# Hashed attention and a gelu feed-forward on one core: new order of the first loads, VectorE's and GpSimd's work spread anew, six banks at the passage, and a branch that falls through

## Chip, cores, metric

The kernel runs on one core of one Trainium2 chip. The metric is the device time of one execution in microseconds (us). Engines are named as the profile names them: PE is TensorE's matmuls, PEld its weight loads, DVE is VectorE, ACT is ScalarE, POOL is GpSimd and SP is SyncE. A "q" behind the name (SPq) is the engine's sequencer, which issues DMAs, branches and waits on semaphores. "Line 310" or L310 is a line of the kernel's source.

## The reference

```python
# attention: 4 batches, 8 heads, 768 positions, head size 64; proj is 64x6
q_bits = (q @ proj) > 0;  k_bits = (k @ proj) > 0          # six bits per row
mask   = bucket(q_bits)[:, None] == bucket(k_bits)[None]   # same bucket only
scores = where(mask, q @ k.T / sqrt(64), -1e9)
attn   = softmax(scores) @ v
# feed-forward: x is 3072 x 512, w_in 512 x 2048, w_out 2048 x 512
h = x @ w_in
out = (h * sigmoid(1.702 * h)) @ w_out
```

## The kernel before

Heads are handled in 16 pairs. For each pair, k and q are fetched, DVE turns them (`kT`, `qT`), PE forms the **hash** (six projections of every row), DVE makes bit features `f` from it, and DMAs spread them into `kf` and `qf`. PE adds the scores of the real rows and of the features, so that pairs in different buckets get a strongly negative score, ACT takes the exponential, PE multiplies by v, and the denominator is a sum of the exponentials, added on POOL and DVE and then summed across partitions by PE (`dn`).

```python
def featured(n, queues):
    f = ...                                     # DVE: hash -> bits
    for i, x in enumerate("kq"):                # k: both halves, then q
        for c in range(2):
            for j in range(2):
                queues[j].dma_start(out=feats[n % 2][x][...], in_=f[...])

def norm(n, c):                                 # one piece, right after dn
    nc.vector.transpose(rt, dn)                 # frees the one small PSUM bank
    nc.vector.reciprocal(r, ...)
    nc.vector.transpose(rt, r.to_broadcast(...))
    nc.vector.tensor_tensor(x_of(n, c), x_of(n, c), rt, op=Alu.mult)
```

Beside attention, one chunk of `w_in` per pair is converted to the form that the feed-forward multiplies (`convert`: a load into one `raw` buffer, then seven DVE operations, with the addition among them on POOL, and a little ACT). The feed-forward forms each block from seven products instead of eight, as in Strassen's scheme. For that it needs sums of quarters of its operands: `in_sums` for `w_in` (they fill `s_in`), `sums_b` for x.

```python
# start of attention, before
fetch(0, "k"); fetch(0, "q", nc.scalar); fetch_v(0)
turn(0, "k"); turn(0, "q")
hashed(0)
featured(0, (nc.sync, nc.scalar))
measure(0, "k"); measure(0, "q")
...
# at the end: a slow path for inputs too large for the exponential
unsafe = nc.values_load(largest[0:1, 0:1].bitcast(I32)) >= SAFE_BITS
with tc.If(unsafe):
    ...
```

## Time and profile before

| | before |
|---|---|
| median of three first runs | 950.01 us (949.92 to 950.5) |
| span of the profiled execution | 948.2 us |
| third hash starts at | 47.62 us |
| last (16th) hash starts at | 324.33 us |
| first product of the feed-forward to the start of its second task | 15.24 us |
| task 4 of the feed-forward | 12.02 us |
| last DVE sum to the end of the span | 8.50 us |

The rows from "third hash" on come from start times in the timeline; they cut the execution into stretches that can be compared between kernels. A task is one block of the feed-forward, seven products on PE. The timed figure is about 2 us above the span of the same execution.

The prediction shows the lines that carry the reading of this profile. One more view belongs beside it: the windows of the kernel before, in the last third of attention. The columns are the window, then each engine's busy time with its number of instructions, the granted clock of PE, and the DMA engines' share and rate.

```profile
core 0: us, PE busy (x) PEld busy (x) DVE busy (x) ACT busy (x) POOL busy (x), PEclk, DMA share, GB/s
255.00:280.00 25.00, 22.74 (x146) 9.42 (x147) 22.83 (x29) 13.28 (x21) 9.39 (x6) 0.93 0.35 72
280.00:305.00 25.00, 22.75 (x152) 10.16 (x150) 22.89 (x29) 14.09 (x22) 10.23 (x7) 0.97 0.36 72
```

PE has gaps of 2.3 us in each 25 us, DVE is busy for almost 23, and the clock is below 1: here, in the last third of attention, PE waits for DVE.

### The profile page before, as it was taken

Reading aid. Unit: us, or ns where it says so; the run is one execution under the profiler, and the core shown is the slowest. Engines: PE = TensorE matmul, PEld = TensorE weight load, DVE = VectorE, ACT = ScalarE, POOL = GpSimd, SP = SyncE. Lnnn points to the kernel's source line nnn. Section 1 sums busy time; section 2 is a strip of 40 time slices with the busy share of each in tenths; the row PEclk is TensorE's granted clock in tenths of the full one; section 3 lists DMA queues with packets and bytes.
Section 4 is the critical chain, followed back from the end, with each engine's and each line's share of the span. In section 5 each row is a group of like instructions: output and inputs, shape, how many; then the busy total and the mean of one; then the engine's idle time right before and its main releaser. Section 6 shows DMA issues by size and latency. Waiting matters only on the chain.

```text
span 948.2 us, 11379 instructions
## 1 busy us (share of the span) xinstructions
PE 916.5 (97%) x4193; PEld 527.7 (56%) x4193; DVE 548.3 (58%) x753; ACT 299.5 (32%) x480; POOL 194.9 (21%) x122
## 2 busy tenths in 40 slices
PE   3999999999899999999999999999999999999996
PEld 1444444444343443444444444447888888888885
DVE  2678878879999788466866687445232314141410
ACT  2756656656565652233233322221000000000000
POOL 2343344345533345011100005300000000000000
PEclk9999999999999999999999999999999999999998
DMA  7533354433333301233333382328242415130101
GB/s 115 91 77 77 78 103 101 95 78 76 76 77 77 73 24 66 106 125 131 130 132 132 133 310 87 112 83 274 77 146 65 157 58 164 56 123 12 34 11 37
DMA packets 178563, 94.32 MB, mean 99 GB/s; under 512 B 129856, under 2 KB 162112, under 8 KB 178496
## 3 DMA queue, kind: packets, MB, share of 16 engines
q1 hardware_dynamic: 175200, 93.05, 34.8%
q10 hardware_dynamic: 3232, 0.43, 0.5%
q8 instruction: 35, 0.57, 0.2%
q14 instruction: 32, 0.26, 0.1%
q0 software_dynamic: 64, 0.00, 0.0%
HBM read 60.82 MB, written 31.46 MB: 97 GB/s over the span
## 4 chain that ended last, share of the span: by engine, by line
PE 87%; DVE 6%; issue 2%; DMA 2%; SPq 1%; ACTq 1%; POOL 0%; ACT 0%; DVEq 0%; POOLq 0%
PE product L630 31%; PE product L588 30%; PE ps L332 13%; PE av L357 10%; PE dn L375 2%; PE hash L305 1%; DVE acc L347 1%; DMA q<-in_q_dram 1%; SPq L315 1%; DVE acc L348 1%; DVE acc L349 1%; DVE kT L288 0%; ACTq L315 0%; DVE qT L288 0%; DMA raw<-in_moe_w_in_dram 0%
## 5 line engine op out<-in xcount | busy, mean ns | idle before, releaser
L334 ACT ACTIVATE e<-ps 128x768 f32<-128x768 f32 x192 | 152.7, 811 | 98.7 <-PE ps L332 93.7
L332 PE MATMUL ps<-qT,kT 64*128 64x384 f32 x768 | 158.6, 493 | 0.0
L357 PE MATMUL av<-e,v 128*64 128x385 f32 x768 | 138.3, 495 | 0.0
L588 PE MATMUL product<-xT,w_in_sb 128*128 128x512 f32 x288 | 135.5, 593 | 0.0
L592 ACT ACTIVATE c<-c 128x512 f32<-128x512 f32 x72 | 45.3, 631 | 181.1 <-DVE c L563 131.1
L559 ACT COPY u<-product 128x512 f32<-128x512 f32 x30 | 17.2, 574 | 249.6 <-PE product L630 242.0
L357 PEld LDWEIGHTS av<-e,v 128*64 128x64 f32 x768 | 49.3, 136 | 81.0 <-issue 80.3
L588 PEld LDWEIGHTS product<-xT,w_in_sb 128*128 128x128 f32 x288 | 54.6, 190 | 69.1 <-issue 61.5
L588 PE MATMUL product<-t_x,s_in 128*128 128x512 f32 x192 | 90.2, 592 | 0.0
L332 PEld LDWEIGHTS ps<-qT,kT 64*128 64x128 f32 x768 | 70.2, 193 | 31.2 <-issue 30.9
L560 DVE TENSOR_TENSOR v<-product,u 128x512 f32<-128x512 f32 x30 | 20.6, 687 | 89.3 <-PE product L630 72.3
L332 PE MATMUL ps<-qf,kf 64*128 64x384 bf16 x384 | 64.2, 331 | 5.1 <-ACT e L334 3.0
L343 POOL TENSOR_TENSOR acc<-e 128x768 f32<-128x768 f32 x32 | 49.3, 1541 | 73.7 <-DVE acc L349 57.2
L630 PE MATMUL product<-t_out,xT 128*128 128x256 f32 x288 | 63.6, 379 | 0.0
L630 PE MATMUL product<-w_out_sb,xT 128*128 128x256 f32 x288 | 63.6, 379 | 0.0
L630 PE MATMUL product<-w_out_sb,w_in_sb 128*128 128x256 f32 x288 | 63.6, 379 | 0.0
L344 POOL TENSOR_TENSOR acc<-acc,e 128x768 f32<-128x768 f32 x32 | 62.0, 1937 | 2.5
L588 PEld LDWEIGHTS product<-t_x,s_in 128*128 128x128 f32 x192 | 36.5, 190 | 45.9 <-issue 45.9
L156 POOL TENSOR_TENSOR w_out_sb<-bits,w_out_sb 128x512 f32<-128x512 f32 x16 | 20.2, 1265 | 191.9 <-DVE w_out_sb L154 161.2
L630 PEld LDWEIGHTS product<-w_out_sb,xT 128*128 128x128 f32 x288 | 54.7, 190 | 7.9 <-issue 0.5
L630 PEld LDWEIGHTS product<-t_out,xT 128*128 128x128 f32 x288 | 54.7, 190 | 7.4
L630 PEld LDWEIGHTS product<-w_out_sb,w_in_sb 128*128 128x128 f32 x288 | 54.7, 190 | 7.4
(103 smaller groups left out, 1121.7 us busy)
## 6 DMA issues: line engine op xcount, KB each, us to landing
g_dram<-c SPq DMA_DIRECT2D x72, 256.0 KB
xT<-g_dram SPq DMA_DIRECT2D x12, 1024.0 KB
w_in_sb<-g_dram SPq DMA_DIRECT2D x12, 1024.0 KB
raw<-in_moe_w_in_dram SPq DMA_DIRECT2D x16, 512.0 KB
raw<-in_moe_w_out_dram SPq DMA_DIRECT2D x16, 512.0 KB
k<-in_k_dram SPq DMA_DIRECT2D x64, 96.0 KB
v<-in_v_dram SPq DMA_DIRECT2D x32, 192.0 KB
g_dram<-u SPq DMA_DIRECT2D x24, 256.0 KB
```

The costliest lines, as they stand in the source:

```text
L156: nc.gpsimd.tensor_tensor(dst, of(bits.bitcast(F32)), dst, op=Alu.add)
L332: nc.tensor.matmul(p[:, j, 0:HS], x[0][hs, keys], x[1][hs, cols], start=first, stop=not first)
L334: nc.scalar.activation(es[c][:, kt, :, 0:HS], p[:, :, 0:HS], Act.Exp, scale=1.0 / D**0.5)
L343: nc.gpsimd.tensor_tensor(acc, e[0], e[1], op=Alu.add)
L344: nc.gpsimd.tensor_tensor(acc, acc, e[2], op=Alu.add)
L357: nc.tensor.matmul(av[D * j : D * (j + 1), :], vt[:, t, j, :], es[c][:, t, j, :], start=(t == 0), stop=(t == T - 1))
L375: nc.tensor.matmul(dn[D * j : D * (j + 1), :], ones, acc[:, j, :], start=True, stop=True)
L559: nc.scalar.copy(u, product(1))
L560: nc.vector.tensor_tensor(v, product(6), u, op=Alu.add)
L588: nc.tensor.matmul(ps, wq[LEFT[i]][:, kc, :], xq[RIGHT[i]][:, kc, :], start=(kc == 0), stop=(kc == K2 - 1))
L592: nc.scalar.activation(c, c, Act.Gelu_apprx_sigmoid)
L630: nc.tensor.matmul(ps[:, m, :], x[:, m * P : (m + 1) * P], wqs[RIGHT[i]][:, c, :], start=(c == 0), stop=(c == FC // 2 - 1))
```

## The change

Its intent is to take PE's gaps away: at the start, in the last third of attention, at the passage to the feed-forward and behind the last instruction. The diff, cut to its core:

```diff
+    nc.scalar.activation(..., Act.Exp)            # a dummy: loads ACT's table early
-        nc.gpsimd.dma_start(out=pb[...], in_=proj)
+        nc.scalar.dma_start(out=pb[...], in_=proj)
 ... convert:
-        nc.gpsimd.tensor_tensor(dst, of(bits.bitcast(F32)), dst, op=Alu.add)
+        nc.vector.tensor_tensor(dst, of(bits.bitcast(F32)), dst, op=Alu.add)
+    LATE = 4                                      # four chunks are converted in the feed-forward
 ...
-    def in_sums(i):                               # halves of w_in: 4 operations of 128x1024
-        return sums_a(nc.gpsimd, *quarters_in(slice(i * CW, (i + 1) * CW)))
+    def in_sums(mt):                              # eight slices: 4 operations of 128x256 each
+        return sums_a(nc.gpsimd, *quarters_in(slice(mt * P, (mt + 1) * P)))
 ... featured:
-                for i, x in enumerate("kq"):
-                    for c in range(2):
+                for c in range(2):
+                    for i, x in enumerate("kq"):
 ... norm is split: invert (transpose, reciprocal) and norm (transpose back, product);
     both now come one group later, invert ahead of the turns
 ... start of attention:
-            fetch(0, "q", nc.scalar)
+            fetch(0, "q", (nc.scalar, nc.gpsimd))
             fetch_v(0)
-            turn(0, "k")
-            turn(0, "q")
+            for x in "kq":
+                turn(0, x)
+                measure(0, x)
+                if last:
+                    fetch(1, x)
             hashed(0)
             featured(0, (nc.sync, nc.scalar))
-            measure(0, "k")
-            measure(0, "q")
+            begin(0, nc.scalar)                   # first chunk's load on ACT's queue
 ... the turns of the next pair: k at step 0, q at step 1 (before: both at step 0)
 ... feed-forward: PSUM banks 4 + 4 become 6 + 2; the late chunks after tasks 1 and 2;
     slice mt + 1 of in_sums after task mt
-    with tc.If(unsafe):
+    with tc.If(unsafe, preferred_fallthrough_block=False):
```

More of the change, by code (lines that the diff above doesn't have):

```diff
@@ L73 @@
     nc.vector.memset(ones, 1.0)
+    nc.scalar.activation(const.tile([1, 1], F32, name="first"), ones[0:1, 0:1], Act.Exp)
     pb = const.tile([P, P], F32, name="pb")
@@ L78 @@
     for j in range(2):
-        nc.gpsimd.dma_start(out=pb[D * j : D * (j + 1), D * j : D * j + NB], in_=proj)
+        nc.scalar.dma_start(out=pb[D * j : D * (j + 1), D * j : D * j + NB], in_=proj)
     def offsets(name, row):
@@ L128, with convert @@
     CW = 512
-    def convert(cv, dst, src):
+    def convert(cv, dst, src, queue=nc.sync):
         raw = cv.tile([P, CW, 2], U32, tag="raw", name="raw")
-        nc.sync.dma_start(out=raw, in_=src)
+        queue.dma_start(out=raw, in_=src)
         def of(x):
@@ L266, in attention, with fetch @@
             raws, vts, xts = {}, {}, {}
-            def fetch(n, name, queue=nc.sync):
+            def fetch(n, name, queues=(nc.sync, nc.sync)):
                 b, hp = pairs[n]
@@ L276, in fetch @@
                         r0 = D * j + 32 * a
-                        queue.dma_start(out=x[r0 : r0 + 32], in_=rows[a])
+                        queues[j].dma_start(out=x[r0 : r0 + 32], in_=rows[a])
             def fetch_v(n):
@@ L375, in total, with invert @@
                     nc.tensor.matmul(dn[D * j : D * (j + 1), :], ones, acc[:, j, :], start=True, stop=True)
-            def norm(n, c):
+            def invert(n, c):
                 dn = accs.pop((n, c))
@@ L384, in norm @@
                 nc.vector.reciprocal(r, rt.rearrange("p (s i) -> p s i", i=32)[:, :, 0:1])
+                accs[n, c] = rt, r
+            def norm(n, c):
+                rt, r = accs.pop((n, c))
                 nc.vector.transpose(rt.rearrange("p (s i) -> p s i", i=32), r.to_broadcast([P, HS // 32, 32]))
@@ L389, in attention, with step, begin @@
             last = len(pairs) - 1
-            conv = [iter(())]
-            def step(count):
+            conv = {}
+            def step(n, count=1):
                 for _ in range(count):
-                    next(conv[0], None)
-            done = XT * 2 // S + (XT * 2 % S > 0)
-            extra = {HP * done + 1: in_sums(0) + sums_b(nc.vector, *quarters_x(0))}
-            rest = []
+                    next(conv.get(n, iter(())), None)
+            def begin(n, *args):
+                if n < min(len(in_chunks) - LATE, last + 1):
+                    conv[n] = convert(cv, *in_chunks[n], *args)
+                    step(n)
+            x_sums = sums_b(nc.vector, *quarters_x(0))
             def guard(part):
@@ L409, in attention @@
             fetch(0, "k")
-            fetch(0, "q", nc.scalar)
+            fetch(0, "q", (nc.scalar, nc.gpsimd))
             fetch_v(0)
-            turn(0, "k")
-            turn(0, "q")
+            for x in "kq":
[3 more added lines that the diff above has]
+                    fetch(1, x)
             hashed(0)
             featured(0, (nc.sync, nc.scalar))
-            measure(0, "k")
-            measure(0, "q")
-            for g in range(len(groups) + 3):
+            begin(0, nc.scalar)
+            for g in range(len(groups) + 4):
                 n, c, kt = groups[g] if g < len(groups) else (last + 1, 0, 0)
@@ L422, in attention @@
                     scores(n, c, range(kt, kt + GT), g > 0)
-                    if at == 0:
-                        for _ in conv[0]:
-                            pass
-                        conv[0] = convert(cv, *in_chunks[n])
-                        step(1)
-                    if n < last and at == 0:
-                        if n == 0:
-                            fetch(1, "k")
-                            fetch(1, "q")
-                        turn(n + 1, "k")
-                        turn(n + 1, "q")
-                        measure(n + 1, "k")
-                        measure(n + 1, "q")
+                if 4 <= g and groups[g - 4][2]:
+                    invert(*groups[g - 4][:2])
+                if n < last and at < 2:
+                    turn(n + 1, "kq"[at])
+                    measure(n + 1, "kq"[at])
+                if 4 <= g and groups[g - 4][2]:
+                    norm(*groups[g - 4][:2])
                 if 1 <= g <= len(groups):
@@ L447, in attention @@
                     fetch_v(n + 1)
-                if 3 <= g and groups[g - 3][2]:
+                if 3 <= g <= len(groups) + 2 and groups[g - 3][2]:
                     total(*groups[g - 3][:2])
-                    norm(*groups[g - 3][:2])
                 if n == last and at in (1, 3):
                     guard(at // 2)
-                if n <= last and at:
-                    step(at + 1 if at > 1 else 2)
-                    if at == 1:
-                        rest += extra.pop(n, [])
-                    if at in (1, 3) and rest:
-                        rest.pop(0)()
+                if at == 0:
+                    step(n)
+                elif at == 2:
+                    step(n, 2)
+                    if n > last - len(x_sums):
+                        x_sums[n - last - 1]()
+                elif at == 3:
+                    step(n, 4)
+                    begin(n + 1)
                 if g == len(groups):
-                    for _ in conv[0]:
-                        pass
-                    assert not rest and not extra
-                    for f in in_sums(1):
+                    for f in in_sums(0):
                         f()
@@ L537, in shifted_attention, with feed_forward @@
                     nc.scalar.copy(xT[:, hp, s0 : s0 + HS], av)
-    def feed_forward(tag):
+    def feed_forward(tag, late=()):
         G2 = XT // 2
@@ L546, in feed_forward @@
             stage = fctx.enter_context(tc.tile_pool(name=f"stage{tag}", bufs=2, side="right"))
-            sets = [fctx.enter_context(tc.tile_pool(name=f"f0{tag}", bufs=4, space=PSUM, side="right"))]
+            late, todo_sums = list(late), []
+            sets = [fctx.enter_context(tc.tile_pool(name=f"f0{tag}", bufs=6, space=PSUM, side="right"))]
             todo, turn = [], [-1]
@@ L554, in product @@
                     turn[0] += 1
-                    ps = sets[turn[0] // 4 % len(sets)].tile([P, XT], F32, tag="p", name="product")
+                    ps = sets[turn[0] % 8 // 6 if len(sets) > 1 else 0].tile([P, XT], F32, tag="p", name="product")
                     mm(i, ps)
@@ L652, in feed_forward @@
                     n = sb * (FC // 2) + mt
-                    if n == 2:
-                        sets.append(fctx.enter_context(tc.tile_pool(name=f"f1{tag}", bufs=4, space=PSUM)))
+                    if n == 1:
                         wop = fctx.enter_context(tc.tile_pool(name=f"wo{tag}", bufs=1))
@@ L660, in feed_forward @@
                         wqs += [t_out[:, i] for i in range(3)]
-                        steps = conversions(cv, [(w_out_sb[:, :, fc, :], wo[fc]) for fc in range(FC)])
+                        steps = conversions(cv, late + [(w_out_sb[:, :, fc, :], wo[fc]) for fc in range(FC)])
+                        todo += [lambda: [next(steps) for _ in range(2 * LATE // 2)]] * 2 if late else []
                         todo += [lambda: (next(steps), next(steps))] * FC
                         todo += sums_b(nc.gpsimd, *wqs)
+                    if n == 2:
+                        sets.append(fctx.enter_context(tc.tile_pool(name=f"f1{tag}", bufs=2, space=PSUM)))
+                        turn[0] = 7
                     if (sb, mt) == (n1 - 1, 0):
@@ L669, in feed_forward @@
                         mid, end = g0[:2], g0[2:]
+                    if sb == 0 and mt + 1 < FC // 2:
+                        todo_sums = in_sums(mt + 1)
                     task(mm, emit, mid, end)
+                    for f in todo_sums:
+                        f()
+                    todo_sums = []
                     yield
@@ L685 @@
     with tc.manual_schedule(engines=ORDERED):
-        ff = feed_forward("")
+        ff = feed_forward("", in_chunks[len(in_chunks) - LATE :])
         attention(ff)
@@ L694 @@
                 whole(convert(cv, *x))
-        for f in in_sums(0) + in_sums(1):
+        for f in in_sums(0):
             f()
```

## The prediction

> **What bounds the kernel now.** I read the page first, then TensorE's own waits, then the timeline around each wait, then the windows for the granted clock. The page:
>
> ```profile
> span 948.2 us, 11379 instructions
> PE 916.5 (97%) x4193; PEld 527.7 (56%) x4193; DVE 548.3 (58%) x753; ACT 299.5 (32%) x480; POOL 194.9 (21%) x122
> ```
>
> TensorE is busy 97% of the span, and the change removes none of its matmuls. All it can win is TensorE's idle time, 948.2 - 916.5 = 31.7 us, plus whatever a low clock stretches. The waits of PE say where 23.1 us of it lie (releaser, total us, times, longest):
>
> ```profile
> PE hash L305 <- DVE kT L288: 9.8, 1, 9.8
> PE hash L305 <- DVE rt L382: 6.2, 4, 2.7
> PE ps L332 <- ACT e L334: 3.0, 1, 3.0
> PE ps L332 <- DMA qf<-f: 2.1, 1, 2.1
> PE product L588 <- DVE v L560: 2.0, 1, 2.0
> ```
>
> Three are the start (9.8, 2.1, 3.0), one the last third of attention (6.2), one the passage to the feed-forward (2.0); the rest, 948.2 - 939.7 = 8.5 us, comes after the last matmul. In the timeline of the start:
>
> ```profile
> 8.37 0.24 DVE L109 TENSOR_SCALAR pf_k<-pb 64x6 f32<-64x6 f32 x2 [0.88 <-DMA pb<-in_proj_dram]
> 8.79 0.98 DVE L288 STREAM_TRANSPOSE kT<-k 128x768 f32<-128x768 f32 x1
> 17.06 1.28 ACT L295 ACT_TABLE_LOAD   x1 [17.06 <-DMA qf<-f]
> 20.17 2.19 ACT L334 ACTIVATE e<-ps 128x768 f32<-128x768 f32 x3
> ```
>
> The reader is to see that k's transpose stands behind the small projection's arrival (its DMA is issued by POOL and takes 5.4 us to land), not only behind k; and that ScalarE, done with DMA issues at 17.0, loads its table and measures k and q before the first exponential, at 20.17. TensorE's second scores wait for that.
>
> In attention a pair of heads takes 20.55 us from hash to hash. From the fifth pair from the end it slips: hashes start at 212.06, 232.97, 256.33, 279.21, 302.09 and 324.33, so the last five intervals are 20.91, 23.36, 22.88, 22.88 and 22.24. Their excess over 20.55 is 9.5 us. The cause is here:
>
> ```profile
> 227.11 2.37 POOL L169 TENSOR_TENSOR w_in_sb<-w_in_sb 128x1024 f32<-128x1024 f32 x1
> 227.29 3.01 DVE L347 SCALAR_TENSOR_TENSOR acc<-e 128x768 f32<-128x768 f32 x1
> 256.33 0.85 PE L305 MATMUL hash<-kT,pf_k 128*32 128x384 f32 x2 [2.74 <-DVE rt L382]
> ```
>
> L347 takes 0.95 us undisturbed; started with a POOL addition under way it takes 3.01. DVE is busy 22.9 of 25 us in the window from 250 us (window 205 to 230: 20.9), and falls behind. The hash needs the one small PSUM bank, which DVE's transpose of the denominator (L382) frees, and that transpose stands in DVE's queue behind two turns and three additions. The hash's 0.85 instead of 0.52 shows that the wait also costs clock: the window from 250 has 0.93 of it, that from 302 has 0.94.
>
> **What the Trainium skill says.** "SBUF — State Buffer", Who interferes with whom: a VectorE instruction with two SBUF inputs and a GpSimd instruction that reads SBUF exclude each other, the later one blocks fully. The trace agrees: 0.95 becomes 3.01. "TensorE: Matmul & The Clock Gate", What's actually happening: the clock is halved after an idle window of about 3.4 us. Here waits of 2.74 and 2.25 us were already followed by half clock, waits of 0.93 and 1.99 not. "DMA: Bandwidth & Descriptors", SWDGE vs HWDGE vs iDMA: DMAs from GpSimd have their descriptors made by software, those of SP and ACT by hardware. The 5.4 us of the projection agree in direction. "Runtime: NRT & Kernel Launch", Instruction fetch mechanics: a taken branch to a far target stalls for the fetch. The trace agrees, below.
>
> **The change part by part.**
>
> *Start.* The projection moves to ACT's queue, the exponential's table is loaded at once by a dummy, the two measurements stand before the hash, the first halves of the bits are sent before the second ones, half of q goes over POOL, the first weight chunk is deferred onto ACT's queue, and the second pair's k and q are fetched as soon as the buffers are free. VectorE gets the projection some 4 us sooner, so kT starts when k lands, before 7 us instead of 8.79. What then counts is q. POOL has its memsets first (until about 4.1 us: it ended at 5.26 with 1.18 us of projection issues that now go), and its DMA took 2.7 us from issue to its first packet for the projection; 768 pieces of 128 B twice may take longer. I put q's landing at 9 us, against qT's start at 9.70: -0.7. From there to bits: of the four DMAs on ACT's queue (13.0, 14.6, 15.5, 16.2 us) the second now suffices instead of the third, -0.8. ACT is free when it has issued its four (4.0 us) and the new chunk (estimate 0.7): the first features at 12.9 - 0.7 = 12.2, so exponentials from 12.2 + 4.7 = 16.9, against 20.17: -3.2. The smaller steps are inside this. The second hash waited another 0.8 us for q of the second pair (1.59 instead of 0.78 in the chain), fetched only at 21.5: -0.8. Start: -4.0.
>
> *Attention.* The four large POOL sums of w_in (2.35 us each) leave for the feed-forward, cut into eight slices; the last four chunks' conversions go there too; each conversion's addition moves from POOL (1.27 us) to DVE (0.69 us). Before, the last step of a conversion waited 1.38 us for POOL and then took 2.02 instead of 0.69 us against the next POOL sum: 1.38 + 1.33 = 2.7 us of DVE per pair, now 0.7. DVE per pair, from its rows: turns 1.9, six additions 5.7, two normalisations 4.2, features 0.7, conversion 4.0, together 16.5 of 20.55 us; POOL's 7 us of additions per pair may add 2 to 3 by exclusion. In the last four pairs the conversion's 4.0 is gone and one x sum (1.2) comes. The release of the small bank also moves forward, ahead of a turn and away from the additions. So I take the whole excess: -9.5, of which 6.2 waits and the rest clock and slower matmuls.
>
> *Passage.* Task 0 of the feed-forward lost about 2.4 us: 372.95 - 357.71 = 15.24 against 12.03 for a task and 0.8 for a denominator. With 6 banks instead of 4 and no 2.4 to 2.9 us additions on DVE, products run through. But the inversion now comes one step later in the order: the first of the last two denominators is transposed only after task 0's last sum, and the second denominator needs its bank. That is one DVE sum 0.69, one transpose 0.58 and about 0.2 of latency: +1.5. Passage: -0.9.
>
> *Late chunks.* Two conversions each after tasks 1 and 2, with one raw buffer. A chunk's reload is issued after the fifth DVE operation (2.7 us in) and lands about 3.3 us later, so two chunks take 6.2 + 4.0 = 10.2 us. Counted from the start of task 2 on TensorE: DVE converts from 0.9 to 11.0, does task 2's sums until 15.9, converts from 15.9 to 26.0. POOL's sums for slice 4 need the last chunk: three of about 0.7 us (estimate: half of 1.27, a little overhead), ready at 28.2. Task 4's second product wants them at 24.06 + 1.72 = 25.8. So a new wait of about +2.5, long enough to lose clock as in attention (1.7 us at the 303 us one), which I weigh by half: +3.4. Eight banks (8 x 1.72 us) hold otherwise.
>
> *Rest of feed-forward.* Conversion of w_out ends one task later, still before its use; additions move to DVE, which is half idle there: 0.
>
> *End.* From the timeline and the branch line:
>
> ```profile
> 939.72 0.69 DVE L572 TENSOR_TENSOR c<-product,c 128x512 f32<-128x512 f32 x1 [6.22 <-PE product L630]
> L691 SPq COMPARE_BRANCH  x1: 45/45/45, 941.4 to 941.4; - x1
> L691 SPq EVENT_SEMAPHORE  x8: 17/17/17, 944.1 to 946.7; - x8
> ```
>
> SP branches at 941.4 and goes on at 944.1; among its eight waits is a second hole, 944.2 to 946.3, in which instruction fetches run. The last output's packets are in by 943.0. If the skipping path is straight on, SP waits for that output until about 943.1 and the closing sequence (946.76 to 948.2, 1.45 us) follows: 944.7 instead of 948.2: -3.5; a jump might remain behind it, so -3.2.
>
> Sum: -4.0 - 9.5 - 0.9 + 3.4 - 3.2 = -14.2, from 950.0 to 935.8.
>
> **Rivals.** (1) DVE stays the bound in attention: the 16.5 us plus exclusion come near 20.55, and the moved addition can now itself be shut out by POOL. For it: L347 and L159 show such losses. Against: before 212 us there was no slip with more DVE time per pair. It would give back 3 to 5 us: 939 to 941. (2) The start gains nothing: q's half on POOL lands at 11 us or later, or the early fetches stand on SP ahead of the bits. Then only table and reordering remain, about -1.5: 938. (3) The late chunks do not bind, because slack I do not see covers 2.5 us: 932.4. (4) The branch keeps a jump: 939.
>
> **Range and chances.** Attention's 9.5 is the surest term, the late chunks and the start the least sure, each by 2 to 3 us either way; the end by 2. Added as independent, about 4 us; so 930.5 to 941.0. Two per cent faster means under about 931.4, which needs rival 3 and a better start together: 0.14. Slower than now by two per cent would need a new stall of over 30 us: 0.01.
>
> **What would show it.** Right: hash intervals of 20.55 throughout and no wait on rt L382 but one of about 1.5 us after task 0; no POOL operation over 2.1 us in attention; the first exponential near 17 us with the table load before 3; a wait of product L588 for POOL's s_in near 410 us; about 4.5 us between the last DVE sum and the end. Wrong: other or longer PE waits in attention, qT later than 10 us, or SP still resuming 2.6 us after its branch. Most of all an error in DVE's order would make me wrong, since every term but the end hangs on it.

## The result, and the profile after

The changed kernel takes 946.07 us (median of six runs, 945.07 to 946.46), and the kernel before 949.96 us (947.9 to 950.5) in the same rounds. The ratio is 0.9962, with a 95% interval of 0.9949 to 0.9975: the same within 2%. A ratio is the mean time of one kernel's fast runs over that of the other's of the same rounds, so it is not quite the ratio of the medians quoted. The prediction was 935.8 us with a range of 930.5 to 941.0: the time lies outside it. All outputs are right.

The page of the changed kernel:

```profile
span 943.7 us, 11414 instructions
PE 916.0 (97%) x4193; PEld 527.6 (56%) x4193; DVE 566.8 (60%) x785; ACT 300.2 (32%) x481; POOL 160.9 (17%) x114
```

POOL has lost 34 us of work and DVE has gained 18.5. The waits of PE (releaser, total us, times, longest):

```profile
PE hash L310 <- DVE kT L293: 7.7, 1, 7.7
PE ps L337 <- DMA qf<-f: 5.3, 1, 5.3
PE product L596 <- POOL s_in L175: 2.5, 1, 2.5
PE hash L310 <- DVE qT L293: 2.4, 1, 2.4
PE dn L380 <- DVE rt L387: 1.4, 1, 1.4
PE ps L337 <- ACT e L339: 0.3, 1, 0.3
```

All four waits for `rt` in attention are gone, and the 3.0 us wait for ACT's exponential at the start has shrunk to 0.3. In their place the wait for the first bits (`qf`) has grown from 2.1 to 5.3. New are one wait of 2.5 for POOL's slice sums, one of 1.4 for `rt` behind task 0, and 2.4 for `qT` of the first pair. The stretches of the table, before and after:

| stretch | before | after | difference | predicted |
|---|---|---|---|---|
| start, to the third hash | 47.62 | 49.18 | +1.6 | -4.0 |
| attention, third to last hash | 276.71 | 267.32 | -9.4 | -9.5 |
| passage, first product to the second task | 15.24 | 14.44 | -0.8 | -0.9 |
| late chunks, task 4 | 12.02 | 16.43 | +4.4 | +3.4 |
| end, last DVE sum to end of span | 8.50 | 8.20 | -0.3 | -3.2 |
| sum (span: 948.2 to 943.7) | | | -4.5 | -14.2 |

Three of the five are right to within about 1 us. The start and the end are not, and they hold 8.5 of the 9.7 us by which the sum misses. Each row is one profiled execution: in the eight kernels here that share the new order of the first loads (the change, e3 to e8 and e10), the third hash starts between 48.73 and 50.27, so the start is known to about 0.8 us either way. The timeline of the start after the change (start, duration, engine, line, operation, tiles, and in brackets the idle time before it with what ended it):

```profile
4.02 1.58 POOL L282 DMA_DIRECT2D q<-in_q_dram  x2
...
7.74 3.96 SPq L282 DMA_DIRECT2D k<-in_k_dram  x4
...
10.62 0.98 DVE L293 STREAM_TRANSPOSE qT<-q 128x768 f32<-128x768 f32 x1 [2.94 <-DMA q<-in_q_dram]
...
12.90 4.65 SPq L282 DMA_DIRECT2D q<-in_q_dram  x4
13.96 1.33 ACTq L320 DMA_DIRECT2D kf<-f  x1
...
18.59 0.90 SPq L320 DMA_DIRECT2D kf<-f  x1
...
21.89 1.15 PE L337 MATMUL ps<-qf,kf 64*128 64x384 bf16 x6 [5.27 <-DMA qf<-f]
...
22.44 2.22 ACT L339 ACTIVATE e<-ps 128x768 f32<-128x768 f32 x3 [10.82 <-PE ps L337]
```

SP first issues the second pair's k and q, and only then its half of the first pair's bits: ACT issues its `kf` at 13.96, SP not before 18.59. The four issues of q start at 12.90, 13.48, 15.99 and 17.25, because in the trace each waits for the completion semaphore of an earlier DMA (a counter that says that this DMA has landed; the next DMA that is to use the same counter must wait for it). SP's waits show on which DMAs of the bits it stood:

```profile
SPq L282 <- DMA kf<-f: 2.2, 1, 2.2
...
SPq L320 <- DMA kf<-f: 0.9, 1, 0.9
...
SPq L282 <- DMA qf<-f: 0.9, 1, 0.9
```

The third and fourth issue of q (L282) stand until ACT's own first two transfers of bits have landed (15.98 and 17.23), and SP's first bits (L320) until ACT's third has (18.51).

The windows of the last third of attention, to be held against those of the kernel before:

```profile
core 0: us, PE busy (x) PEld busy (x) DVE busy (x) ACT busy (x) POOL busy (x), PEclk, DMA share, GB/s
255.00:280.00 25.00, 25.00 (x170) 10.78 (x164) 20.16 (x29) 15.67 (x24) 6.83 (x4) 1.00 0.32 56
280.00:305.00 25.00, 25.00 (x168) 10.88 (x166) 17.93 (x23) 15.43 (x25) 11.38 (x6) 1.00 0.30 54
```

PE has no gap, the clock is full, and DVE has 5 to 7 us to spare. The late chunks, in the timeline of the feed-forward (task 2 starts on PE at about 376.4, task 4 at 400.5):

```profile
383.43 0.43 DVE L146 TENSOR_SCALAR sign<-raw 128x512 uint32<-128x512 uint32 x1 [1.99 <-DMA raw<-in_moe_w_in_dram]
...
398.26 0.43 DVE L146 TENSOR_SCALAR sign<-raw 128x512 uint32<-128x512 uint32 x1 [1.95 <-DMA raw<-in_moe_w_in_dram]
...
401.78 0.69 DVE L161 SCALAR_TENSOR_TENSOR w_in_sb<-size,w_in_sb 128x512 f32<-128x512 f32 x1
402.55 0.73 POOL L173 TENSOR_TENSOR s_in<-w_in_sb 128x256 f32<-128x256 f32 x1 [45.19 <-DVE w_in_sb L161]
...
404.03 0.73 POOL L175 TENSOR_TENSOR s_in<-s_in,w_in_sb 128x256 f32<-128x256 f32 x1
404.81 3.68 PE L596 MATMUL product<-t_x,s_in 128*128 128x512 f32 x4 [2.46 <-POOL s_in L175]
```

The second chunk of each two waits about 2 us for the single `raw` buffer to be loaded again; the last one is done at 402.5; POOL's third sum ends at 404.8, and PE starts then. The four matmuls after this wait take 3.68 us instead of 1.88: the clock has halved, for 3.4 us in the records.

The end, in the lines of the branch (durations in ns, then the first and last start):

```profile
L707 SPq EVENT_SEMAPHORE  x8: 17/17/17, 937.3 to 939.5; - x8
...
L707 SPq COMPARE_BRANCH  x2: 42/46/49, 937.2 to 939.5; - x2
```

After the branch at 937.2 SP goes on at once (937.3), where before it went on 2.7 us later. But there are now two branches: the second, at 939.5, is the jump over the slow path, right behind the last of the eight semaphore waits. The span ends 4.2 us after it. SP's next instruction after the jump starts at 942.25, so 2.7 us of this are the jump; the rest is the closing sequence, 1.45 us as before.

### The profile page after: what moved, and what is told of

Its sections match the earlier page's. It is cut to its first block, busy times and chain, and to the rows that moved or that the text cites. A ratio compares the mean times of both kernels' runs of the same rounds, so it can differ in the third digit from the quotient of the medians.

```text
span 943.7 us, 11414 instructions
## 1 busy us (share of the span) xinstructions
PE 916.0 (97%) x4193; PEld 527.6 (56%) x4193; DVE 566.8 (60%) x785; ACT 300.2 (32%) x481; POOL 160.9 (17%) x114
## 4 chain that ended last, share of the span: by engine, by line
PE 56%; DVE 1%; DMA 0%; POOL 0%; issue 0%; DVEq 0%; SPq 0%
PE product L638 31%; PE product L596 25%; DMA raw<-in_moe_w_in_dram 0%; DVE w_in_sb L156 0%; DVE bits L149 0%; DVE c L580 0%; DVE sign L152 0%; DVE sign L146 0%; POOL s_in L173 0%; POOL w_in_sb L174 0%; DVE w_in_sb L161 0%; DVE w_in_sb L158 0%; DVE c L569 0%; DVE bits L147 0%; POOL s_in L175 0%
## 5 line engine op out<-in xcount | busy, mean ns | idle before, releaser
L348 POOL TENSOR_TENSOR acc<-e 128x768 f32<-128x768 f32 x32 | 55.8, 1743 | 224.1 <-DVE acc L354 179.5
L349 POOL TENSOR_TENSOR acc<-acc,e 128x768 f32<-128x768 f32 x32 | 55.1, 1721 | 2.5
L337 PEld LDWEIGHTS <-kf 64*128 64x128 bf16 x384 | 19.0, 95 | 61.3 <-issue 38.0
```

What stands on the lines that cost most here:

```text
L337: nc.tensor.matmul(p[:, j, 0:HS], x[0][hs, keys], x[1][hs, cols], start=first, stop=not first)
L348: nc.gpsimd.tensor_tensor(acc, e[0], e[1], op=Alu.add)
L349: nc.gpsimd.tensor_tensor(acc, acc, e[2], op=Alu.add)
```

## The experiments

Each starts from the changed kernel unless said otherwise. The time before was 950.5 us in the rounds of e1 to e4, 950.48 in those of e5, e7, e8 and e9, and 948.39 in those of e6, e10 and the two repaired versions, so ratios, not times, are to be compared across them.

| run | us | ratio to before (95%) |
|---|---|---|
| the change | 946.07 | 0.9962 (0.9949 to 0.9975) |
| e1 second pair's fetch behind the bits | 943.43 | 0.9938 (0.9919 to 0.9957) |
| e2 all of first q on ACT | 948.61 | 0.9989 (0.9969 to 1.0009) |
| e3 two raw buffers | 940.47 | 0.9904 (0.9886 to 0.9923) |
| e4 branch as before | 946.18 | 0.9963 (0.9944 to 0.9983) |
| e5 no late chunks | 941.91 | 0.9919 (0.9903 to 0.9936) |
| e6 conversion's addition on POOL | 1004.66 | 1.0581 (1.0563 to 1.0599) |
| e7 inversion as before | 949.85 | 1.0000 (0.9983 to 1.0016) |
| e8 four large sums back in attention | 946.75 | 0.9970 (0.9951 to 0.9988) |
| e9 second pair's fetch on POOL's queue | 943.75 | 0.9928 (0.9904 to 0.9953) |
| e10 taken branch, far target | 944.13 | 0.9947 (0.9929 to 0.9964) |
| b1 repaired | 936.36 | 0.9857 (0.9838 to 0.9876) |
| b2 repaired, and e10's branch | 934.31 | 0.9842 (0.9827 to 0.9857) |

### The start: e1, e2, e9

The theory: SP's early fetches stand ahead of SP's bits. The rival: POOL's half of q, which lands 1.5 us later than predicted, is the loss.

**e1** issues the second pair's fetch after the bits.

```diff
                 measure(0, x)
-                if last:
-                    fetch(1, x)
             hashed(0)
             featured(0, (nc.sync, nc.scalar))
+            for x in "kq" if last else ():
+                fetch(1, x)
```

> The changed kernel with one thing moved: the early fetch of the second pair's k and q comes after the first pair's bits in program order. Theory (the early fetches stand in front of the bits on SP's queue, so that the bits land at 21.9 us instead of about 17): bits at about 17, first exponential near 18.3 instead of 22.4, third hash near 45 instead of 49.2, time 4 us under the changed kernel's 946, so about 942. Rival A (half of q over POOL is what costs the start): first exponential stays at 22 or later than 21, gain under 1 us. Rival B (the second pair's data come too late again): the first exponential moves, but the second hash waits by as much, gain under 1.5 us.

Measured, in its timeline:

```profile
13.82 0.90 SPq L320 DMA_DIRECT2D kf<-f  x1
...
18.37 2.22 ACT L339 ACTIVATE e<-ps 128x768 f32<-128x768 f32 x3 [6.87 <-DMA qf<-f]
```

SP sends its first bits at 13.82 instead of 18.59 and the first exponential starts at 18.37 instead of 22.44, as the theory had it. The third hash starts at 45.67, 3.5 us earlier than in the changed kernel; the time gained 2.3 us (0.9962 to 0.9938), less than the 4 expected. Part of the gain is lost again. The second pair's rows now come late, and its hash waits 1.08 us for `qT`. In the third pair `qT` is done only at 46.47, when the hash of k has begun; the two hashes then run one after the other, 1.62 us instead of 0.78, and the interval to the fourth hash is 21.39 instead of 20.55. The early fetch was no mistake in itself; its place in SP's queue was.

**e2** takes the rival's suspect away.

```diff
-            fetch(0, "q", (nc.scalar, nc.gpsimd))
+            fetch(0, "q", (nc.scalar, nc.scalar))
```

> The changed kernel with all of the first q on ACT's queue instead of half on POOL's. Theory (SP's order is the main loss, POOL's half a smaller one): q lands near 8 instead of 10.6, but the bits still wait for SP's fetches; first exponential 1 to 2.5 us earlier than 22.4, time 944 to 945. Rival (POOL's half is the loss): exponential near 18, time about 942.

The result goes against both numbers. q is turned earlier (9.76 against 10.62), but the first scores of the bits come later (23.27 against 21.89), and the third hash starts at 51.48. In the trace's records of the DMAs the ones of SP and ACT share eight completion semaphores, and POOL's have two of their own. With q's other half on ACT, one more pair of DMAs takes shared semaphores, and the turn of each later DMA moves on. SP's first bits leave at 18.74, about as before, but its `qf` leaves at 21.27 instead of 19.59: its semaphore is now that of the first weight chunk, issued by ACT at 16.80 and landed at 21.20. In this order of issues POOL's half therefore saves some 2 us (51.48 against 49.18, with the start known to 0.8), although it lands late.

**e9** leaves the early fetch in its place but moves it to POOL's queue.

```diff
-                    fetch(1, x)
+                    fetch(1, x, (nc.gpsimd, nc.gpsimd))
```

> The changed kernel with the early fetch of the second pair's k and q left early, but issued by POOL, which is idle then, instead of SP. Theory (SP's queue, held up by its waits for free DMA semaphores, is what delays the bits): bits near 17 and first exponential near 18.3 as with the fetch moved behind the bits, and the second pair's data by 22, so that the second and third hash don't wait either: third hash near 44.7 instead of 49.2, time 941 to 942. Rival (the transfers themselves, or POOL's slower descriptors, hold the bits or the second pair up): third hash at 46 or later, time 943 to 946.

SP's first bits leave at 14.03 and the first exponential starts at 18.55, so with another cure the same illness is gone. What the transfers cost on POOL's queue can be read from its issues of q:

```profile
12.24 2.83 POOL L282 DMA_DIRECT2D q<-in_q_dram  x4 [1.33 <-ACT junk L300]
```

By the semaphores in the trace these four DMAs landed between 15.85 and 17.63, so the rival's reason, slow transfers, is not borne out. `qT` of the second pair starts only at 23.82 for another reason: in DVE's queue the conversion of the first weight chunk stands ahead of it, and that waited 5.40 us for its chunk, until 21.66. PE lost nothing by it, since the second hash starts at 25.73 without idle time before it. The third starts at 45.63 instead of the 44.7 expected, and the time, 943.75 (940.99 to 944.98), lies in the rival's range; I don't know what holds the last microsecond. Together e1 and e9 show that the early fetch on SP costs the start some 3.5 us, and e2 that POOL's half of q isn't the loss.

### The end: e4, e10

**e4** takes the branch as before.

```diff
-    with tc.If(unsafe, preferred_fallthrough_block=False):
+    with tc.If(unsafe):
```

> The changed kernel with the branch as before (no preferred fall-through). Theory (the fall-through only exchanges a taken conditional branch for a jump behind the last wait: after the last VectorE sum the end took 8.5 us before and 8.2 now): the end takes 8.2 to 8.6 us again, time 946.0 to 946.5. Rival (it did save something that the layout of instructions took back): 3 us longer, 949.

The ratio is 0.9963 against 0.9962: no difference. Its lines of the branch:

```profile
L707 SPq EVENT_SEMAPHORE  x8: 17/17/17, 941.0 to 943.8; - x8
...
L707 SPq COMPARE_BRANCH  x1: 45/45/45, 938.4 to 938.4; - x1
```

Here is one branch, 2.6 us to the first wait, and a second hole of 2.2 us among the eight waits (941.2 to 943.4). The first hole lies beside the landing of the last output, which is waited for anyway; the changed kernel has no hole there, but the jump comes after that landing, in the open.

**e10** keeps the taken branch and pads the head of the slow path with 24 tiny loads that are never run, so that the target lies farther on.

```diff
-    with tc.If(unsafe, preferred_fallthrough_block=False):
+    with tc.If(unsafe):
+        with tc.tile_pool(name="pad", bufs=1) as pp:
+            far = pp.tile([1, 24], F32, name="far")
+            for i in range(24):
+                nc.sync.dma_start(out=far[0:1, i : i + 1], in_=proj[i : i + 1, 0:1])
```

> The changed kernel with the branch as before, and 24 small loads added on SP at the head of the slow path, which never runs; they only move the place of the instructions to which SP jumps. Theory (the taken branch has two parts: a fetch of 2.6 us, mostly hidden behind the last output's landing, and a second hole of 2.2 us[...]): the second hole goes, the end takes 6.3 to 6.6 us from the last VectorE sum instead of 8.2 (fall-through) and 8.6 (taken branch unpadded), time about 944. Rival (the second hole is no matter of the place): the end stays at 8.2 to 8.8, time 946.

```profile
L707 SPq EVENT_SEMAPHORE  x8: 17/17/17, 939.7 to 940.2; - x8
...
L707 SPq COMPARE_BRANCH  x1: 45/45/45, 937.1 to 937.1; - x1
```

The branch still costs 2.6 us, but the eight waits now follow within 0.5 us: the second hole is gone, and the end takes 6.33 us instead of 8.20, and instead of 8.61 in e4, from which only the target's place differs. Why the place matters isn't shown; the run shows only that moving the target removes the hole. The gain is read from the trace: the ratios of e10 and e4 (0.9947 and 0.9963) have intervals that overlap.

### The late chunks: e3, e5

**e3** gives the feed-forward's conversions two `raw` buffers.

```diff
-        raw = cv.tile([P, CW, 2], U32, tag="raw", name="raw")
+        raw = cv.tile([P, CW, 2], U32, tag="raw", name="raw", bufs=raws)
...
-                gens = [convert(cv, *x) for x in chunks]
+                gens = [convert(cv, *x, raws=2) for x in chunks]
```

> The changed kernel with two raw buffers for the conversions inside the feed-forward instead of one. Theory (the stall of 4.4 us at task 4 comes from waiting twice 2.0 us for a reload of the single raw buffer): both waits of VectorE go, the last late chunk is done about 4 us sooner (22 instead of 26 us after task 2's start), POOL's third sum is ready near 24.3, before TensorE wants it at 25.8, so task 4 takes 12.0 instead of 16.4 us, time about 941.6. Rival (VectorE simply has too much work there, or the loads are slower with two in flight): task 4 keeps 1 to 4 us of it, time 943 to 945.5.

Task 4 takes 12.01 us, the wait for `s_in` is gone, and with it 0.58% of the time (0.9962 to 0.9904), some 5.5 us, of which task 4 explains 4.4. The reload of the one buffer was the cause.

**e5** converts all chunks in attention.

```diff
-    LATE = 4
+    LATE = 0
```

> The changed kernel with no late chunks: all sixteen conversions of w_in inside attention again, the sums still in slices in the feed-forward. Theory (after the other parts VectorE has room, so that the late chunks cost 4.4 us and buy nothing): hash intervals stay at 20.55 to 20.7 in the last four pairs, task 4 takes 12.0 us, time 941 to 942. Rival (the last four pairs need the relief, with conversion 4.0 and an x sum of 1.2 us each): intervals of 21 to 22.5 there, 2 to 6 us in sum, time 943 to 947.

Task 4 takes 12.01 here too. In attention only the last interval grows, to 21.21, by 0.66. So moving the four chunks bought at most 0.7 us and cost 4.4: of the two ways to undo the loss, e3 keeps the gain.

### Attention: e6, e7, e8

These undo one of attention's parts each.

**e8** puts the four large POOL sums back.

```diff
+            half_sums = sums_a(nc.gpsimd, *quarters_in(slice(0, CW)))
...
+                if 9 <= n <= 10 and at in (1, 3):
+                    half_sums.pop(0)()
```

(with the first slices of the feed-forward left out in exchange)

> The changed kernel with the first half of the sums of w_in again on POOL inside attention, four of 2.35 us at the old places in pairs 9 and 10; the rest stays changed. Theory (exclusion between those large sums and VectorE's additions made VectorE late): additions of 2.5 to 3 us beside them, hash intervals longer by 0.3 to 3 in pairs 9 to 11, time 1 to 4 us over the changed kernel. Rival (VectorE has so much room now that four sums are absorbed): intervals unchanged, time 945.5 to 946.5.

The two pairs take 21.26 and 21.73 us instead of 20.55, +1.9 together. The timeline shows how:

```profile
222.48 2.68 POOL L174 TENSOR_TENSOR w_in_sb<-w_in_sb 128x1024 f32<-128x1024 f32 x1
...
222.86 2.85 DVE L156 SCALAR_TENSOR_TENSOR w_in_sb<-raw,sign 128x512 f32<-128x512 uint32 x1
```

L156 takes 0.69 us undisturbed; started with POOL's sum under way it takes 2.85 and ends 0.55 after it. The theory's 1 to 4 us hold for attention. The time moved by only 0.7. In the profiled execution the clock didn't drop at task 4 (15.09 us instead of 16.43), and the four executions fall in two groups: 945.93 and 946.21 with a mean clock of 0.995, 947.29 and 947.60 with 0.992. The changed kernel's six lie between 945.07 and 946.46, all with 0.991 to 0.993; against executions of that clock, e8 is some 1.5 us slower.

**e6** moves the conversion's addition back to POOL.

```diff
-        nc.vector.tensor_tensor(dst, of(bits.bitcast(F32)), dst, op=Alu.add)
+        nc.gpsimd.tensor_tensor(dst, of(bits.bitcast(F32)), dst, op=Alu.add)
```

> The changed kernel with each conversion's addition on POOL again instead of VectorE. Theory (the large sums, not this addition, made VectorE late; there was no slip before them with the addition on POOL): hash intervals stay at 20.55 to 20.7; in the late chunks each conversion takes some 0.6 us more, so task 4 takes 16.5 to 19 us; time 946 to 949. Rival (the move of the addition carries attention): intervals of 20.7 to 21.5 in the pairs with a conversion, 2 to 8 us in sum, time 949 to 954.

Some 58 us slower than the changed kernel: both expectations fell. Attention lost 2.2 us (seven intervals of 20.86 instead of 20.55). The rest is in the feed-forward, in the first of PE's waits:

```profile
PE product L596 <- POOL s_in L175: 46.2, 6, 12.2
```

POOL takes its instructions in order. The additions of the conversions that run between the tasks stand ahead of the next slice's sums, and each of them waits for DVE; so the slices come late, tasks last 20 to 27 us instead of 12, and the idle PE loses clock (mean 0.968). Moving the addition to DVE was thus no gain to be counted apart: slicing the sums on POOL needs it.

**e7** inverts and normalises right after the denominator, as before.

```diff
                     total(*groups[g - 3][:2])
+                    invert(*groups[g - 3][:2])
+                    norm(*groups[g - 3][:2])
```

(and no calls one group later)

> The changed kernel with inversion and normalisation at their old place, right after the denominator. Theory (the earlier release of the small bank is not what freed attention; VectorE's smaller load is): intervals stay at 20.55 to 20.7; at the passage the wait of 1.4 us for the bank goes, as the first denominator is transposed before task 0's sums; time 944 to 945. Rival (the order is what counts): waits of the hash for the transpose of the denominator return in the last four to six pairs, 2 to 6 us, time 946 to 950.

The time is back at that of the kernel before. The passage is faster, as expected: 13.01 us instead of 14.44, with the 1.4 us wait of `dn` gone. But each of the ten intervals from the fourth to the 14th hash is about 21.06, 0.5 more. The rival had named the amount but not the place: in the last pairs there are no waits. Nor does the list of PE's waits show this 0.5; the timelines of DVE and PE do:

```profile
217.74 0.96 DVE L293 STREAM_TRANSPOSE qT<-q 128x768 f32<-128x768 f32 x1
...
218.25 0.84 PE L310 MATMUL hash<-kT,pf_k 128*32 128x384 f32 x4
218.76 0.84 PE L310 MATMUL hash<-qT,pf_q 128*32 128x384 f32 x4
```

`qT` is done at 218.70, after the hash of k has begun. The hash of q follows that of k instead of running beside it, and the two take 1.28 us (until 219.53) instead of 0.78 (the same hash in the changed kernel, 213.67 to 214.45). The same shows in e5's last interval (1.44) and e6's long ones (1.09). `qT` is late because the turn of q comes one step later in the change than before, directly ahead of the hash that needs it, and here the whole normalisation, waiting for its `dn`, stands before that turn in DVE's queue. So the changed order of inversion and normalisation is what pays for the later turn. It has its price at the passage, where there is no turn to make room for.

### Two repaired versions: b1, b2

**b1** puts together what the runs taught: POOL's half of q ahead of its memsets, the second pair's k early on POOL's queue and its q on SP behind the bits, the first weight chunk on ACT ahead of the bits, two `raw` buffers, and the first of the last two denominators inverted before task 0. Its edit, cut to its core:

```diff
-            for e in es: nc.gpsimd.memset(...)         # these go behind
-            for f in feats: nc.gpsimd.memset(...)      #   fetch(0, "q", ...)
...
                 measure(0, x)
-                if last:
-                    fetch(1, x)
+                if last and x == "k":
+                    fetch(1, x, (nc.gpsimd, nc.gpsimd))
+            begin(0, nc.scalar)
             hashed(0)
             featured(0, (nc.sync, nc.scalar))
+            if last:
+                fetch(1, "q")
...
                 if g == len(groups):
+                    invert(*groups[g - 3][:2])
+                    norm(*groups[g - 3][:2])
```

> A mended version of the changed kernel: POOL issues its half of the first q before its memsets and the early fetch of the second k, the second q is fetched behind the bits, the first weight chunk is issued on ACT before the bits, the first of the last two denominators is inverted before task 0's sums, and the late chunks have two raw buffers; the branch stays as changed. Theory: first exponential near 15.5 to 16.5 (q lands near 8), third hash at 41.5 to 43 instead of 49.2; wait for the bank gone, passage 13.0 instead of 14.4; task 4 12.0 instead of 16.4; 6.5 + 1.4 + 4.4 = 12 us under the changed kernel, about 934. Rival (the gains at the start eat each other, since the second pair's data become the next wait): third hash at 44 or later, time 936 to 938.

936.36 us. `qT` starts at 8.52, as meant, but the bits were ready at 17.09 and the third hash at 45.23, not 41.5 to 43: the rival's start came true. Task 4 takes 12.02 and the passage 13.01. The stretches add up: -2.4 start, -9.3 attention, -2.2 passage, 0 for task 4 and for the end, -13.9 as in the profile (948.2 to 934.3).

**b2** is b1 with the padded, taken branch of e10.

> The mended version with the padded taken branch in addition. Theory: 1.7 to 1.9 us under it, about 932, ratio to before 0.981. Rival: the place of the jump's target is wrong here again and the end takes 8.2 to 8.8 us, time as without.

934.31 us, the fastest of all, faster than both kernels in question, though by 1.6% and so still within 2% of the one before. The end takes 6.52 us. Its waits of PE show what is left at the start:

```profile
PE hash L305 <- DVE kT L288: 8.1, 1, 8.1
PE ps L332 <- DMA qf<-f: 3.4, 1, 3.4
PE ps L332 <- ACT e L334: 0.6, 1, 0.6
```

These 12 us are all that the list of PE's waits holds. In b1 `f` was made at 11.8, and the first half's bits, issued between 11.85 and 13.49, landed between 16.58 and 17.17. ACT's `qf` took 3.7 us from issue to landing, where it took 1.9 in the changed kernel. The second pair's k on POOL's queue was landing until 16.60; no run separates whether that is the reason, so it stays open.

## Why the prediction was wrong, and where it was right

**Start: wrong by 5.6 us; this step failed first.** The step reads "ACT is free when it has issued its four (4.0 us) and the new chunk (estimate 0.7): the first features at 12.9 - 0.7 = 12.2, so exponentials from 12.2 + 4.7 = 16.9". Two terms in it are off. q landed at 10.5 instead of 9 (in the kernel before, with all of it on ACT, it was in at 8.8), so the features were ready at 13.87. And the 4.7 us from there to the exponentials counted ACT's queue only, where SP carries the other half: with eight fetches ahead of it, SP sent its first bits 4.7 us after `f` was ready (18.59 - 13.87), and the exponential came at 22.44. The issues alone don't fill this time: the four of q take 0.31 us each, so from 12.90 on they alone would have been through at about 14.2 (an estimate). What filled it were waits for completion semaphores, which SP shares with ACT, in the end those of ACT's own bits; this is read from the traces, no run changes the sharing alone. I had looked for the gain of the earlier fetch (0.8) and never laid SP's queue end to end, with what each issue waits for. Rival 2 named the cause, "the early fetches stand on SP ahead of the bits", but gave it a gain of 1.5; measured is a loss of 1.6. e1 and e9 show the cause. The smaller points held: `kT` began at 6.70, and the table's load lay before 3 us and beside nothing that mattered.

**Attention: right.** -9.5 predicted, -9.4 measured; all intervals are between 20.55 and 20.61, and no wait for `rt` and no half clock are left. The experiments qualify the reason. The prediction gave DVE's collisions with POOL's large sums most weight; e8 shows the collision (0.69 to 2.85 us) but only 1.9 us for it. e6 gives 2.2 for the addition, e5 0.7 for the late chunks, and e7 shows 0.5 us in each of ten intervals, 4.9 in all, for the order of inversion and normalisation, but as the price of the later turn of q and not as the old slip. No single undoing brings the old slip back, and they needn't add: the sum was right, and how the 9.4 us divide among the parts is not settled.

**Passage: right.** -0.9 predicted, -0.8 measured, with the new wait of 1.4 us (1.5 predicted); e7 and b1 recover it.

**Late chunks: the mechanism right, the size 1.0 too small.** The conversions were to end 26.0 us after task 2's start and did so at 26.03; POOL's third sum was to be ready at 28.2 and was at 28.3; the wait was to be 2.5 and was 2.46. The mis-sized term is the clock, weighed by half: 0.9 predicted, 16.43 - 12.02 - 2.46 = 1.95 measured in the profiled execution. In the profiles of e1 and e8, with waits of 2.91 and 2.81, it wasn't paid at all; in those of the change, e2, e4, e7, e9 and e10 it was. So a weight was the right form, and a half was low.

**End: wrong by 2.9 us; the second step that failed.** The step reads "a jump might remain behind it, so -3.2": a jump did remain, and it was sized at 0.3 where it costs 2.7. It stands behind the wait for the last output. Of the two old holes, the first (2.6) lay mostly beside that wait and the second (2.2) in the open; so the change took away one open hole of 2.2 us and put one of 2.7 in its place. Rival 4 said that a jump stays and put it at 939 alone. e4 shows that the branch's part of the change is worth no more than the 0.4 us by which the ends differ (8.61 and 8.20).

With rivals 2 and 4 both true, as they were, the prediction's own figures give 935.8 + 2.5 + 3.2 = 941.5, already outside its range; the range had treated start and end as errors that may fall either way.

Two small figures of the prediction are off and change nothing: 943.1 + 1.45 is 944.6 and not 944.7, and the projection's first packet came 3.0 us after its issue (1.98 to 4.98), not 2.7.

## What to carry to other kernels

When a transfer is issued earlier, write down the whole order of that queue, with every issue's duration and what each issue waits for, up to the next transfer that the critical path needs: a fetch for later that stands ahead of it delays it. When a stall is to be removed at the end of a program, ask first what it lies beside: one that overlaps a wait costs nothing, and a fall-through that ends in a jump puts it into the open. When work moves between engines, check the order of each engine's instructions in every stage where that work runs, since e6 cost 58 us in a stage that the move wasn't aimed at.

## What the Trainium skill lacked or had wrong

- "DMA: Bandwidth & Descriptors", Anatomy of one DMA — SWDGE (gpsimd) path, says that any semaphore wait happens on the issuing sequencer before dispatch. The trace agrees and shows what the page doesn't say: a queue whose next DMA needs a completion semaphore still in use holds up everything behind it. Four issues of q stood at 12.90, 13.48, 15.99 and 17.25, and the bits behind them left at 18.59. SP and ACT share eight such semaphores in this program, and POOL has its own (two in the change, eight in e9); I found no page that warns of this.
- The same page, SWDGE vs HWDGE vs iDMA, calls the hardware path faster in setup, without a figure there for DMAs like these. The projection's two landed 5.1 and 5.7 us after their issue by POOL (kernel before) and 3.8 after their issue by ACT (the change). But four of q with 768 pieces each landed 3.3 to 3.6 us after their issue by POOL (e9), hardly later than the same from SP (3.1 to 3.5, kernel before).
- "TensorE: Matmul & The Clock Gate", What's actually happening, gives the half clock after at least one idle window of about 3.4 us. Here it followed a wait of 2.46 us (four matmuls in 3.68 instead of 1.88 us; the half clock lasted 3.41 us), and did not follow one of 2.91 us (e1: 1.98 us).
- "Runtime: NRT & Kernel Launch", Instruction fetch mechanics, says that a taken branch to a far target stalls, without a size. On SP it was 2.5 to 2.7 us, for the conditional branch and for the jump over the skipped block alike, and a second hole of 2.2 us followed the taken branch until the target was moved (e4, e10).
